# Operand sums of a fused attention and gated-FFN kernel put into other slots, and the products that read them started five slots later

## The chip, the cores and the metric

The kernel runs on one core of one Trainium2 chip. The metric is the device time of an execution in microseconds; the median of several runs counts.

## The reference, cut to what matters

```python
B, N, C = (4, 6016, 256)                      # attention over channels
qn = q / (np.linalg.norm(q, axis=1, keepdims=True) + 1e-06)
kn = k / (np.linalg.norm(k, axis=1, keepdims=True) + 1e-06)
s = kn.transpose(0, 2, 1) @ qn / tau          # 256 x 256 scores of a batch
a = np.exp(s - s.max(-1, keepdims=True))
a /= a.sum(-1, keepdims=True) + 1e-09
x = (v @ a).reshape(B * N, C)                 # 24064 tokens, d_ff = 1536
gate = 1.0 / (1.0 + np.exp(-(x @ w_gate)))
out = (gate * (x @ w_val)) @ w_out
```

## The kernel before, in words

The rows of a batch are 47 tiles of 128 (NT), taken as 12 chunks of four tiles (the last has three). For each batch the kernel needs the softmaxed 256 x 256 scores first. It multiplies them into the gate and value weights (`gh`, tiles gh_G and gh_H), so that each chunk of transposed v goes straight to the gate and value products.

A chunk has 12 **slots**, one for each block f of 128 of the 1536 hidden columns. A slot is a pass through `glu`: TensorE computes ps_gate and ps_val (two matmuls of 512 columns each), ScalarE takes the tanh of ps_gate into g_sb (L681), and VectorE forms hT from g_sb and ps_val (L682). ps_gate and ps_val have two buffers each. In the same slot `run_work` issues a twelfth of the output product of the chunk before. That product is done with seven block products in place of eight, in the manner of Strassen; its left operands are sums of blocks of hT, formed on VectorE by `a_sum` (L704). The tables `OWN_SLOTS` and `NEXT_SLOTS` name their slots: 7 to 11 of the chunk itself and 1, 3, 4, 5 and 6 of the next. Slots 0 and 2 have none. ScalarE copies a finished output product out of its bank (L758, L765), and GpSimd (POOL) adds its blocks up (L759, L760, L775, L776).

While batch b runs through its 12 x 12 slots, `side_work(b)` hangs the preparation of batch n = b + 1 onto them: `at(slot, ...)` places a call after the work of that slot, counted from the start of the batch. For n = 1 the scores are plain products. For n = 2 and 3, prepared while batches 1 and 2 run, they too are done with seven products in place of eight, in six **groups** of eight row tiles (the last has seven), 16 slots apart; s0 is the first slot of a group (0, 16, 32, 48, 64, 80).

- `load_qk` loads a group's q and k (tile qk_sb, four buffers) 24 slots ahead, from POOL's queue.
- `score_sums` forms the operand sums of a group, tiles qs0 to qs4. m = 0, 2, 3 and 4 run on VectorE (L351, L359, L364), each with one buffer; m = 1 is a copy by DMA (L355) and an adding DMA (`score_sum_q`, L369), with two buffers.
- `queue_scores` puts the group's products (28, or 25 in the last group; 128 columns each) on a list, and `run_scores` issues them over the next 16 slots: one in each of the first four slots, then two. They go into two PSUM banks, ps_s0 and ps_s1 (bank 0 and 1), in the order of the products: the first two to bank 0, then three to bank 1, then two to bank 0.
- `acc_square`, `acc_add` and `acc_fold` (L297, L308, L315) gather the squares for the norms.

After slot 98 of the batch come the end steps of the scores: `score_out` copies a bank to sm_sb on ScalarE (L426), `norms_mm` writes the norms into the free region of bank 1, and `root_seed`, `norms_inv`, `score_blocks`, `exps` and `gh` follow.

The order of every engine's instructions is the order in which the program issues them; nothing is scheduled again. The functions that the change touches, and their callers:

Of the kernel before, what the change touches and what calls it, by code (L numbers as in the profile page):

```python
# [46 lines left out]
    (1, "x2"), (1, "y2"), (1, "z2"), (1, "v2"),  # L47
)
NEXT_SLOTS = {1: 1, 3: 3, 4: 2, 5: 0, 6: 4}
OWN_SLOTS = {7: 1, 8: 3, 9: 2, 10: 0, 11: 4}  # L50


@with_exitstack
def kernel(
# [31 lines left out]
    FC = DFF // P  # L86
# [77 lines left out]
    t0, nt = groups0[0]  # L164
# [528 lines left out]
    def a_sum(b, ci, g, m):  # L693

        nt = groups[ci][1]
        half = nt // 2
        hT = hts[b, ci]
        if (b, ci, g) not in sums:
            sums[b, ci, g] = spool.tile(
                [P, len(A_SUMS), FC // 4, CH // 2], BF16, tag=f"s{g}", name="sums", bufs=2 - g  # L700
            )
        (r0, k0), op, (r1, k1) = A_SUMS[m]
        f0, f1 = g * (FC // 2), (g + 1) * (FC // 2)
        nc.vector.tensor_tensor(  # L704
            out=sums[b, ci, g][:, m, :, : half * P],
            in0=hT[:, f0 + k0 : f1 : 2, ds(r0 * half * P, half * P)],
            in1=hT[:, f0 + k1 : f1 : 2, ds(r1 * half * P, half * P)],
            op=op,
        )
# [94 lines left out]
    def run_work(work, share):  # L804

        upto = sum(w[0] for w in work) * share
        done = 0
        while work and done < upto:
            cost, fn, *args = work.pop(0)
            fn(*args)  # L810
            done += cost

    def store():
        while stores:
            b, ci = stores.pop(0)
            t0, nt = groups[ci]
            nc.sync.dma_start(out=out_rows[b][:, t0 : t0 + nt, :], in_=ffn.pop((b, ci))[:, :nt, :])
# [112 lines left out]
    def side_work(b):  # L930


        side = {}

        def at(slot, fn, *a):
            side.setdefault(divmod(slot, FC), []).append((fn, a))

        for ci in range(NCH):
            nb, nci = (b, ci + 1) if ci + 1 < NCH else (b + 1, 0)
            lb, lci = (b, ci + 2) if ci + 2 < NCH else (b + 1, ci + 2 - NCH)  # L940
            if nb < B:
                at(ci * FC + 2, transpose_v, nb, nci)
            if lb < B:
                at(ci * FC + (10 if (b, ci) == (0, 0) else 0), load_v, lb, lci)
            if (b, ci) == (0, 0):
                for i in range(FC // TPC):
                    at(8, copy_w_out, i)
                for n, m in enumerate((1, 0, 3, 2, 4)):
                    for i in range(FC // TPC):
                        at(11 + 2 * n, sum_w_out, m, i)  # L950
        n = b + 1
        if n == B:
            return side
        first, last = (14 if b == 0 else 0), 8 * FC
        wide = [(t, min(2 * TPC, NT - t)) for t in range(0, NT, 2 * TPC)]
        at(first, acc_start, n)
        for g, (t0, nt) in enumerate(groups if b == 0 else []):
            s0 = first + g * (last - first) // NCH
            at(max(FC - 3, s0 - 12), load_qk, n, t0, nt)
            for u in range(nt):  # L960
                at(first + (t0 + u) * (last - first) // NT, score, n, t0, u)
            for w in range(2):
                at(s0 + 1 + 4 * w, narrow_square, n, g, w)
                slot = s0 + 3 + 4 * w
                at(slot + 2 if w == 0 and slot % FC == 8 else slot, narrow_add, n, g, w)
        step = (last - first) / len(wide)
        for g, (t0, nt) in enumerate(wide if b else []):
            s0 = first + int(g * step)
            halves = [(0, nt - TPC), (TPC, TPC)]
            if s0 >= 24:  # L970
                at(s0 - 24, load_qk, n, t0, nt)
            for i in range(4):
                at(s0 + 3 * i, acc_square, n, t0, 1 - i // 2, halves, i % 2)
            for w in range(2):
                at(s0 + 11 - 6 * w, acc_add, n, t0, w, halves)
            for m in (0, 2, 3, 4):
                at(s0 + 3 * max(0, m - 1), score_sums, n, t0, m, halves)
            ahead = 0 if g == 0 else 5
            at(s0 + 1 - ahead, score_sums, n, t0, 1, halves)
            at(s0 + 6 - ahead, score_sum_q, n, t0, halves)  # L980
            end = first + int((g + 1) * step) + 3
            at(s0 + 3, queue_scores, n, t0, halves)
            for slot in range(s0 + 3, end):
                at(slot, run_scores, s0 + 3, end, slot)
        if n + 1 < B:
            for g, (t0, nt) in enumerate(wide[:2]):
                at(NCH * FC - 24 + 16 * g, load_qk, n + 1, t0, nt)
        s0 = 8 * FC + 2
        if b == 0:
            at(s0, acc_fold, n, 0, (2, 1))  # L990
            at(s0 + 1, acc_fold, n, 1, (2, 1))
            at(s0 + 3, norms_mm, n)
            at(s0 + 4, root_seed, n)
            at(s0 + 4, root_steps, n)
            at(s0 + 10, norms_inv, n)
            at(s0 + 11, spread_both, n)
            at(s0 + 13, read_row, n)
        else:
            at(s0 - 3, acc_fold, n, 1, (4,))
            at(s0 - 2, acc_fold, n, 1, (2, 1))  # L1000
            at(s0, acc_fold, n, 0, (4,))
            at(s0 + 2, acc_fold, n, 0, (2, 1))
            at(s0 + 5, score_out, n, 0)
            at(s0 + 6, norms_mm, n)
            at(s0 + 7, score_out, n, 1)
            at(s0 + 7, root_seed, n)
            at(s0 + 7, root_steps, n)
            at(s0 + 12, norms_inv, n)
            at(s0 + 12, spread_both, n)
            at(s0 + 14, read_row, n)  # L1010
            at(s0 + 14, score_blocks, n)
        at(s0 + 22, scale_x, n, 0)
        at(s0 + 24, scale_x, n, 1)
        at(s0 + 25, exps, n, 0)
        at(s0 + 26, exps, n, 1)
        at(s0 + 28, all_sums, n)
        at(s0 + 28, gh_tiles, n)
        for i, piece in enumerate(gh_order):
            slot = s0 + 29 + 2 * i
            if slot < NCH * FC:  # L1020
                at(slot, gh, n, piece, *((pss, "s"), (psm, "m"))[i % 2])
            else:
                spill.setdefault((n, *divmod(slot - NCH * FC, FC)), []).append((gh, (n, piece, psm, "m")))
        return side
# [12 lines left out]
    for b in range(B):  # L1037
        side = side_work(b)
        for ci in range(NCH):
            final = (b, ci) == (B - 1, NCH - 1)  # L1040
            for f in range(FC):
                mid = gh_mid.get(f) if (b, ci) == (0, 0) else None
                glu(b, ci, f, None if mid is None else (lambda: gh_pieces(mid)))
                if prev is not None:
                    if f == 4:
                        store()
                    if f + final in NEXT_SLOTS and prev != (0, 0):
                        a_sum(*prev, 1, NEXT_SLOTS[f + final])
                    run_work(work, 1 / max(1, FC - final - f))
                if f in OWN_SLOTS and not final and (b, ci) != (0, 0):  # L1050
                    a_sum(b, ci, 0, OWN_SLOTS[f])
                for fn, a in spill.get((b, ci, f), []) + side.get((ci, f), []):
                    fn(*a)
                if (b, ci) == (0, 0):
                    gh_pieces(gh_end.get(f, ()))
            prev = (b, ci)
            if not final:
                work = out_work(*prev)
# [39 lines left out]
```

## Time and profile before

| | us |
|---|---|
| median of 4 runs | 802.71 |
| lowest and highest | 800.45, 806.15 |
| the profiled execution, its own time | 800.45 |
| its span, first to last instruction | 798.7 |
| TensorE matmul busy | 778.7 (97%) |
| VectorE (DVE) busy | 712.9 (89%) |
| ScalarE (ACT) busy | 525.3 (66%) |
| GpSimd (POOL) busy | 398.6 (50%) |

Times in the profile are in microseconds from the first instruction, unless marked ns. Batch 1 runs from about 229.6 to 421.5 us and batch 2 to 613.4 us; these are the two in which the changed steps lie. The chain of work that ended last is followed back from the last instruction; in order of time its pieces have a start, a duration and what ran. A matmul's own duration contains its latency, so matmuls overlap in the trace; in the chain each counts only up to the start of the next. PE stands for TensorE, PEld for its weight loads, SP for SyncE.

### The profile page before, as it was taken

What the parts mean: (1) busy time and instruction counts of PE and PEld (TensorE: products, weight loads), DVE (VectorE), ACT (ScalarE), POOL (GpSimd) and SP (SyncE); (2) the same over time, 40 slices, a digit from 0 to 9 for tenths busy, and PEclk for the clock granted to TensorE, in tenths of its full rate; (3) what the DMA queues carried; (4) which work ended last, traced back from release to release, by engine and by line L of the source; (5) the groups of instructions that cost most, each with busy time, mean ns of one, the idle gap of its engine ahead of it and who ended that gap; (6) DMA issues with size and microseconds to landing.
All of it is one profiled execution on the core that took longest, in us unless ns stands there. A gap on an engine that the chain in (4) does not pass through costs nothing.

```text
span 798.7 us, 18203 instructions
## 1 busy us (share of the span) xinstructions
PE 778.7 (97%) x6861; PEld 498.0 (62%) x6875; DVE 712.9 (89%) x1228; ACT 525.3 (66%) x891; POOL 398.6 (50%) x618
## 2 busy tenths in 40 slices
PE   3899999999999999999999999999999999999998
PEld 2556666666666666666666666666666566666666
DVE  5768999999979999999988999999998898998996
ACT  3766777766667767676667777766666566665664
POOL 3565545446453566565843565655744244444433
PEclk9999999999999999999999999999999999999999
DMA  9997758532777899882577599967234323423402
GB/s 213 201 199 133 131 95 139 94 67 54 134 141 143 168 173 165 184 139 54 111 135 152 127 177 192 180 130 135 58 63 86 67 55 80 75 60 72 82 27 74
DMA packets 82776, 95.16 MB, mean 119 GB/s; under 512 B 52512, under 2 KB 58528, under 8 KB 82688
## 3 DMA queue, kind: packets, MB, share of 16 engines
q0 software_dynamic: 25616, 55.85, 39.8%
q1 hardware_dynamic: 56496, 37.30, 21.2%
q8 instruction: 53, 0.87, 0.4%
q10 hardware_dynamic: 576, 0.85, 0.3%
q14 instruction: 35, 0.29, 0.1%
HBM read 79.04 MB, written 24.64 MB: 130 GB/s over the span
## 4 chain that ended last, share of the span: by engine, by line
PE 95%; DMA 4%; issue 0%; DVE 0%; ACT 0%; POOL 0%; DVEq 0%; POOLq 0%
PE ps_gate L129 31%; PE ps_val L129 31%; PE ps_o L129 28%; DMA qk_sb<-in_k_dram 4%; PE ps_s L129 4%; PE ps_gh L129 2%; PE ps_end L129 0%; PE ps_n L129 0%; DVE x_sb L543 0%; PE ps_r L129 0%; ACT e_sb L561 0%; POOL qk_sb L148 0%; DVE x_sb L555 0%; DVE end L839 0%; DVE r L526 0%
## 5 line engine op out<-in xcount | busy, mean ns | idle before, releaser
L681 ACT ACTIVATE g_sb<-ps_gate 128x512 f32<-128x512 f32 (+1 forms) x576 | 337.9, 589 | 224.4 <-PE ps_gate L129 213.9
L682 DVE SCALAR_TENSOR_TENSOR hT<-g_sb,ps_val 128x512 bf16<-128x512 f32 (+1 forms) x576 | 385.4, 670 | 67.3 <-ACT g_sb L681 52.4
L129 PE MATMUL ps_gate<-vT,gh_G 128*128 128x512 bf16 (+1 forms) x1152 | 337.6, 375 | 0.1
L129 PE MATMUL ps_val<-vT,gh_H 128*128 128x512 bf16 (+1 forms) x1152 | 337.5, 375 | 0.0
L704 DVE TENSOR_TENSOR sums<-hT 128x768 bf16<-128x768 bf16 (+1 forms) x460 | 283.3, 616 | 0.0
L129 PEld LDWEIGHTS <-sums 128*128 128x128 bf16 x2670 | 183.0, 98 | 82.0
L129 PEld LDWEIGHTS <-gh_H 128*128 128x128 bf16 x1152 | 112.7, 98 | 130.8 <-issue 0.5
L775 POOL TENSOR_TENSOR out_sb<-out_sb,m_sb 128x256 f32<-128x256 f32 x89 | 79.0, 887 | 187.8 <-ACT out_sb L765 164.7
L129 PE MATMUL ps_o<-w_sums,sums 128*128 128x128 bf16 x1602 | 154.3, 219 | 0.0
L129 PEld LDWEIGHTS <-hT 128*128 128x128 bf16 x1200 | 88.3, 98 | 46.8
L759 POOL TENSOR_TENSOR m_sb<-m_sb 128x128 f32<-128x128 f32 x89 | 45.7, 513 | 126.5 <-ACT m_sb L758 126.1
L129 PEld LDWEIGHTS <-gh_G 128*128 128x128 bf16 x1152 | 92.5, 98 | 12.2 <-DVE gh_G L629 0.3
L129 PE MATMUL ps_o<-w_out_sb,sums 128*128 128x128 bf16 x1068 | 96.2, 219 | 0.0
L129 PE MATMUL ps_o<-w_sums,hT 128*128 128x128 bf16 x1068 | 95.5, 219 | 0.0
L776 POOL TENSOR_TENSOR out_sb<-out_sb 128x256 f32<-128x256 f32 x89 | 76.0, 854 | 7.0
L765 ACT COPY out_sb<-ps_o 128x512 f32<-128x512 f32 x89 | 52.2, 586 | 11.1 <-PE ps_o L129 8.8
L760 POOL TENSOR_TENSOR m_sb<-m_sb 128x128 f32<-128x128 f32 x89 | 55.8, 627 | 7.0
L129 PE MATMUL ps_s<-qk_sb 128*128 128x256 bf16 (+1 forms) x194 | 34.8, 298 | 15.5 <-DMA qk_sb<-in_k_dram 8.6
L758 ACT COPY m_sb<-ps_o 128x384 f32<-128x384 f32 x89 | 42.6, 479 | 3.6 <-PE ps_o L129 1.1
L257 ACT ACTIVATE sq<-qk_sb 128x1024 bf16<-128x1024 bf16 (+3 forms) x36 | 35.6, 1009 | 12.0 <-DMA qk_sb<-in_k_dram 11.9
L297 ACT ACTIVATE sq<-qk_sb 128x1024 bf16<-128x1024 bf16 (+1 forms) x40 | 41.2, 1031 | 0.2 <-DMA acc<-sq 0.2
L129 PEld LDWEIGHTS <-qk_sb 128*128 128x128 bf16 x286 | 27.0, 104 | 21.3 <-issue 10.2
(102 smaller groups left out, 443.4 us busy)
## 6 DMA issues: line engine op xcount, KB each, us to landing
out_dram<-out_sb SPq DMA_DIRECT2D x43, 512.0 KB, 3.4
v_sb<-in_v_dram POOLq DMA_DIRECT2D x44, 256.0 KB, 5.4
acc<-sq POOLq DMA_DIRECT2D x16, 512.0 KB, 8.0
qk_sb<-in_q_dram POOLq DMA_DIRECT2D x14, 512.0 KB, 10.3
qk_sb<-in_k_dram POOLq DMA_DIRECT2D x14, 512.0 KB, 8.4
qs<-qk_sb POOLq DMA_DIRECT2D x20, 256.0 KB, 5.2
qk_sb<-in_q_dram POOLq DMA_DIRECT2D x15, 256.0 KB, 4.7
qk_sb<-in_k_dram POOLq DMA_DIRECT2D x15, 256.0 KB, 6.9
```

Of the source, the lines that this page charges most:

```text
L129: nc.tensor.matmul(out, lhsT=lhsT, rhs=rhs, start=start, stop=stop, **kw)
L257: nc.scalar.activation(out=sq[:, :nt, :], in_=src[:, :nt, :], func=ACT.Square)
L297: nc.scalar.activation(out=s["sq", w][:, u0 : u0 + n, :], in_=src[:, u0 : u0 + n, :], func=ACT.Square)
L681: nc.scalar.activation(out=g_sb[:, :n], in_=ps_gate[:, :n], func=ACT.Tanh, scale=0.5)
L682: nc.vector.scalar_tensor_tensor(out=hts[b, ci][:, f, :n], in0=g_sb[:, :n], scalar=1.0, in1=ps_val[:, :n], op0=ALU.add, op1=ALU.mult,)
L704: nc.vector.tensor_tensor(out=sums[b, ci, g][:, m, :, : half * P], in0=hT[:, f0 + k0 : f1 : 2, ds(r0 * half * P, half * P)], in1=hT[:, f0 ...
L758: nc.scalar.copy(m, states[p]["ps"][:, : 3 * P].rearrange("p (n c) -> p n c", c=P))
L759: nc.gpsimd.tensor_tensor(out=m[:, 1, :], in0=m[:, 1, :], in1=m[:, 2, :], op=ALU.add)
L760: nc.gpsimd.tensor_tensor(out=m[:, 2, :], in0=m[:, 1, :], in1=m[:, 0, :], op=ALU.add)
L765: nc.scalar.copy(o[:, p : p + half + 1 : half, :], states[p]["ps"].rearrange("p (t c) -> p t c", c=C),)
L775: add(out=ends, in0=ends, in1=states[p]["m"][:, 1:3, :], op=ALU.add)
L776: add(out=ends, in0=ends, in1=mids, op=ALU.subtract)
```

## The change: three tables and offsets

It moves steps to other slots. A new table `SCORE_SLOTS`, chosen by the group's s0 modulo 12, gives the slots after s0 of the VectorE sums m = 0, 2, 3, 4; before they were at 0, 3, 6 and 9 after s0 in every group. A group's score products are queued and issued from slot s0 + 8 on, in place of s0 + 3, again over 16 slots. At the end of a batch's scores, bank 1 is copied out at slot 103 and bank 0 at slot 105, in place of the other order; `norms_mm` stays between them. The DMA steps (m = 1, loads, the adding of squares) stay where they are.

```diff
+SCORE_SLOTS = {0: (0, 2, 12, 14), 4: (2, 8, 10, 13), 8: (4, 6, 9, 12)}
...
-            for m in (0, 2, 3, 4):
-                at(s0 + 3 * max(0, m - 1), score_sums, n, t0, m, halves)
+            for m, slot in zip((0, 2, 3, 4), SCORE_SLOTS[s0 % FC]):
+                at(s0 + slot, score_sums, n, t0, m, halves)
             ahead = 0 if g == 0 else 5
             at(s0 + 1 - ahead, score_sums, n, t0, 1, halves)
             at(s0 + 6 - ahead, score_sum_q, n, t0, halves)
-            end = first + int((g + 1) * step) + 3
-            at(s0 + 3, queue_scores, n, t0, halves)
-            for slot in range(s0 + 3, end):
-                at(slot, run_scores, s0 + 3, end, slot)
+            end = first + int((g + 1) * step) + 8
+            at(s0 + 8, queue_scores, n, t0, halves)
+            for slot in range(s0 + 8, end):
+                at(slot, run_scores, s0 + 8, end, slot)
...
-            at(s0 + 5, score_out, n, 0)
+            at(s0 + 5, score_out, n, 1)
             at(s0 + 6, norms_mm, n)
-            at(s0 + 7, score_out, n, 1)
+            at(s0 + 7, score_out, n, 0)
```

In the last hunk s0 is 98, not a group's first slot.

## The prediction

> **What bounds the kernel now.** I read the busy shares first, then the chain of work that ended last, then what TensorE waited for.
>
> ```profile
> PE 778.7 (97%) x6861; PEld 498.0 (62%) x6875; DVE 712.9 (89%) x1228; ACT 525.3 (66%) x891; POOL 398.6 (50%) x618
> ...
> PE 95%; DMA 4%; issue 0%; DVE 0%; ACT 0%; POOL 0%; DVEq 0%; POOLq 0%
> ```
>
> The second line is the one that counts: 95% of the chain is TensorE work and 4% the first loads. DVE is 89% busy and has 0% of the chain. The waits of TensorE (who waited for what; us in total, times, longest) are all in the head of the run, before 37 us:
>
> ```profile
> PE ps_s L129 <- DMA qk_sb<-in_k_dram: 8.6, 6, 3.1
> PE ps_s L129 <- ACT qk_sb L195: 6.9, 1, 6.9
> PE ps_r L129 <- ACT e_sb L561: 0.7, 1, 0.7
> PE ps_rk L129 <- DVE r L527: 0.3, 1, 0.3
> ```
>
> The same question for 229 to 600 us, the two batches that the change touches, is answered with no row. Matmul ends are modelled, so a short stall can hide in a long matmul. I therefore compared pieces of the chain (start, duration, what) slot by slot. This is the worst chunk, 326.99 to 343.4 us:
>
> ```profile
> 328.36 0.43 PE ps_gate L129 x2
> 328.79 0.43 PE ps_val L129 x2
> 329.22 0.39 PE ps_o L129 x7
> 329.61 0.11 PE ps_s L129 x2
> ...
> 331.95 0.39 PE ps_o L129 x7
> 332.34 0.03 issue
> 332.37 0.27 PE ps_s L129 x2
> 332.64 0.43 PE ps_gate L129 x2
> 333.08 0.48 PE ps_val L129 x2
> ```
>
> A normal slot is 0.43 + 0.43 + 0.39 + 0.11 = 1.36 us. The slot from 331.09 has 0.03 of issue and a score piece of 0.27 in place of 0.11; the next val pair has 0.48 in place of 0.43: 0.24 us lost. The cause is on DVE, in the timeline:
>
> ```profile
> 330.53 1.79 DVE L364 TENSOR_TENSOR qs<-qk_sb 128x1024 bf16<-128x1024 bf16 x1
> ...
> 332.24 1.27 DVE L682 SCALAR_TENSOR_TENSOR hT<-g_sb,ps_val 128x512 bf16<-128x512 f32 x2
> ```
>
> An operand sum ran 1.79 us while two POOL adds (L775 at 330.74, L776 at 331.84) were active, the L682 behind it came late, and ps_val, which has two buffers, was not free. Stepping from gate pair to gate pair through both batches I find one more such place, 0.18 us near 518 us, and twice 0.05 us near 232 and 424 us. That is **0.5 us in all**. The check: seven chunks from 245.8 to 359.5 us last 16.24 us each; their work is 48 matmuls of 512 columns (24 pairs x 0.433 = 10.39), 84 output products (12 x 0.39 = 4.70) and some 21 score products (21 x 0.056 = 1.18), together 16.27. There is no room for more.
>
> **What the Trainium skill says.** "Perfetto Trace Analysis", Identifying the Most-Contended Engine: matmul busy share is no measure of distance from the limit. The trace agrees: a 512-column matmul has a mean of 375 ns in its row, yet a pair advances the chain by 0.43 us. "TensorE: Matmul & The Clock Gate", Back-to-back issue gap: the isolated gap is N/2.4 + 2.5 ns, 216 and 56 ns here; the trace has 0.43/2 and 0.39/7, so TensorE issues at that rate. (The same section's lower sustained figure for 512 columns, and its higher one for 128, don't show here.) "SBUF — State Buffer", Who interferes with whom: a DVE instruction with two SBUF inputs contends with a GpSimd instruction that reads SBUF. The trace agrees: these rows span a factor of 2.6 between median and longest, while L682, which has one input in PSUM, stays at a mean of 670.
>
> ```profile
> L364 DVE TENSOR_TENSOR qs<-qk_sb x28: 351/678/1794, 240.9 to 544.9; 128x1024 bf16<-128x1024 bf16 x20, 128x384 bf16<-128x384 bf16 x4, 128x512 bf16<-128x512 bf16 x4
> L351 DVE TENSOR_TENSOR qs<-qk_sb x12: 682/885/1217, 231.7 to 532.2; 128x1024 bf16<-128x1024 bf16 x10, 128x768 bf16<-128x768 bf16 x2
> L359 DVE TENSOR_TENSOR qs<-qk_sb x12: 677/684/1081, 235.8 to 536.4; 128x1024 bf16<-128x1024 bf16 x10, 128x768 bf16<-128x768 bf16 x2
> ```
>
> **The change, part by part.** No instruction is added or removed. The built order of POOL and SP, with all their DMA issues, is the same before and after; on ACT only two pairs of copies change places.
>
> 1. *Operand sums (52 DVE instructions).* Net time on DVE, start to start: L682 0.61 (237.68 to 238.29 us), an L704 sum of the output product 0.47 (330.06 to 330.53), a score sum 0.60 (240.95 to 241.55). A slot with L682 and L704 takes 1.08 of 1.36: 0.28 spare. With a score sum on top it takes 1.68: DVE falls 0.32 behind and catches up in little over a slot. In slots 0 and 2 of a chunk, which have no L704, a score sum makes 1.21: still 0.15 spare. By the tables, score sums in such slots go from 4 to 16 of 24 a batch; the other 8 stay beside an L704 (slots 5, 6, 8). So DVE's lag goes down. DVE isn't on the chain, so this is worth only the stalls that the lag causes: at most 0.24 + 0.18 us. Some can come back elsewhere: slot 92 of a batch now holds L682, L704 and two short score sums (0.61 + 0.47 + 0.27 + 0.34 = 1.69), and an acc fold follows in slots 95, 96 and 98 (0.60 net for its long step). By the same adding, the lag there peaks near 0.35 us, some 0.4 more with a POOL add over it, under the cushion of L682. That cushion is 1.2 us: L681 starts 0.2 us after its gate pair, so 0.63 into a slot, takes 0.60, L682 0.03 later takes 0.68, done at 1.94; the ps_val that needs its buffer starts two slots on, at 2 x 1.36 + 0.43 = 3.15. Value taken: -0.3 us; ends -0.5 and +0.7 (three stalls of the worst size seen).
>
> 2. *Score products five slots later (330 matmuls).* The same products at 0.056 us each, so 0 in sum. In a batch's first five affected slots some 6 products (0.34 us) go missing and the end has them instead. Cover: in slots 3 to 7 DVE also loses two score sums (1.2 us), so it isn't squeezed; in slots 99 to 103 TensorE has 0.06 to 0.11 us a slot more, which gives DVE time. Do operands come in time? run_scores takes one product in each of the first four slots, then two. The sum m=4 is first used 16 slots into its group and made at 12, 13 or 14 (before: 11 and 9): at least two slots, 2.7 us, as before. m=0 has 4 or more, m=2 6, m=3 4. The POOL-issued DMAs for m=1 gain five slots. Buffers: qs0 is next written at slot 16 and last read at 13; a qk_sb tile is last read at 23 and loaded again at 40. No wait appears; cost 0.
>
> 3. *Copies swapped.* Bank 0 now gets its last product in slot 103 and is copied in 105; bank 1 is complete by slot 100 and copied in 103. L426 (0.47 to 0.58 us) waits for nothing before. New is that norms_mm, which writes bank 1 in slot 104, waits for the copy of slot 103. Behind it on TensorE stands all of slot 105. Price: ACT starts the gate's L681 some 0.2 us after the pair, takes 0.59, then the copy 0.5: done 1.3 us after the pair's end, while norms_mm comes 2.2 us after it or later. Cost 0; if ACT were held up by a whole copy, 0.1 to 0.5 us, twice.
>
> Sum: -0.3 + 0 + 0 = **-0.3 us** on the profiled execution of 800.45 us (span 798.7 and 1.75 around it). That execution is the fastest of the four shown and 0.3% under their median of 802.71; against the median I say 802.4.
>
> **Rivals.**
>
> *A, no change* (above): 802.4, between 801.5 and 803.5 by its own costs, wider by the scatter of runs.
>
> *B, faster.* The median is 2.3 us above the profiled run. If that gap is the same DVE stall in other executions, the change could take it too: 800.4, or -0.3%. For it: such stalls depend on where POOL adds fall, and that can vary. Against: the trace shows only 0.5 us of them, and TensorE's sum of work leaves no others. Past -0.5% (4 us) nothing in the trace reaches.
>
> *C, slower: the sums meet POOL.* Slots 0 and 2 are where the second pair of POOL adds (L775, L776) runs, for its ACT copy ends as a chunk begins: from 230.05 to 231.58 us in the chunk at 229.8, and from 330.74 in the one at 326.99. A score sum wholly beneath them takes 1.1 us longer. One hit in slot 0 or 2 puts DVE 0.95 behind, inside the cushion of 1.2; two, in slots 0 and 2 of one chunk, make 0.95 - 0.28 + 0.95 = 1.6, and 0.4 us stall. In all twelve groups that is 4.8 us: 807.5. It decides once both sums of a chunk are hit. Against: the pair lasts 1.5 to 2.2 us and the two slots lie 2.7 us apart, so mostly one is hit; and before, too, POOL adds met score sums.
>
> *D, it doesn't do what it says*: a third of the score sums still stand beside an L704, and the old stalls stay: 802.7.
>
> **How the numbers follow.** About 0.5% (4 us) is what a measurement of this kernel can tell from no change. A 0.73 and D 0.10 lie within it; B 0.09, of which 0.03 for a time past 4 us from a cause unseen; C 0.08, of which 0.05 past 4 us and 0.03 with only some chunks hit. So faster 0.03, same 0.73 + 0.10 + 0.06 + 0.03 = 0.92, slower 0.05. The range takes B's 800.4 and half of C, and the scatter of the four runs (800.45 to 806.15): 799.8 to 805.8.
>
> **What the profile after would show.** Right: TensorE still 95% of the chain; chunks of 16.2 us through both batches; L364's longest well under 1.79 us or without a late L682 behind it; no TensorE wait for L426. Wrong: a row of TensorE waiting for hT L682, qs or sm_sb; score-batch chunks longer than 16.4 us; or the whole chain shorter by more than 0.5 us, which would mean that TensorE's matmul spacing itself had changed.

## The result, and the profile after

The changed kernel takes 803.56 us (median of 35 runs, 802.72 to 807.72); the kernel before takes 801.93 us in 56 runs (799.85 to 806.15). The ratio is 1.0024, with a 95% interval of 1.0017 to 1.0031: **slower by some 1.9 us** (the medians as they stand differ by 1.6). The time is within the forecast range and within the 0.5% that was called no change, but it moved the other way from the forecast gain, and clear of the noise.

The profiled execution of the changed kernel has a span of 802.5 us. These are the busy shares and the shares of the chain of work that ended last:

```profile
PE 781.6 (97%) x6861; PEld 498.5 (62%) x6875; DVE 716.3 (89%) x1228; ACT 525.4 (65%) x891; POOL 396.7 (49%) x618
...
PE 89%; DVE 4%; DMA 4%; issue 1%; POOL 1%; ACT 0%; DVEq 0%; POOLq 0%
```

The busy line says next to nothing: 97% as before. The chain says it: VectorE, which had 0%, has 4%, and TensorE went from 95% to 89%. (A share of the chain is not a loss: 4% of it is 32 us.) The waits of TensorE and of its weight loads in the two batches (231 to 617 us; total, times, longest), where the kernel before had no row for matmuls and 0.6 us for weight loads, are:

```profile
PEld L131 <- issue: 3.7, 7, 0.6
PE ps_val L131 <- DVE hT L684: 1.8, 6, 0.4
PEld L131 <- DVE sums L706: 1.1, 4, 0.4
```

(The change adds two lines near the top of the file, so L684 is the former L682, L706 the former L704, L366 the former L364.) Stepping from one chunk's first gate product to the next, as the prediction did, gives nearly the whole of it. From the first gate product of batch 1 to that of batch 3 pass 383.80 us before and 386.29 after. After the change the stalls are in the same places of both batches, all but one:

| us lost by TensorE (slots counted from 0) | before, batch 1 / 2 | after, batch 1 / 2 |
|---|---|---|
| chunk 0, slot 2 | 0.05 / 0.05 | 0.05 / 0.05 |
| chunk 3, slot 3 | - | 0.11 / - |
| chunk 3, slot 11 | - | 0.34 / 0.34 |
| chunk 5, slot 11 | - / 0.18 | - |
| chunk 6, slots 3 and 4 | 0.24 / - | - |
| chunk 7, slot 11 | - | 0.51 / 0.51 |
| chunk 8, slot 2 | - | 0.51 / 0.50 |
| sum of both | 0.5 | 2.9 |

So the old stalls went, as forecast, and larger ones came. The profiled execution also reached batch 1 1.4 us later (231.0 in place of 229.6 us), 1.0 us of it lost in slots 1 and 3 of batch 0, where the listed waits are for the load of w_gate; a second profile of the same kernel (below) didn't.

How the stall at the end of chunk 3 arises can be read in VectorE's timeline (start, duration). The group with s0 = 32 has its m=4 sum in slot 44 of the batch, slot 8 of chunk 3, behind an L706. VectorE runs more than a slot behind TensorE, so its work of slots 8 and 9 falls into TensorE's slots 9 to 11:

```profile
291.67 0.68 DVE L684 SCALAR_TENSOR_TENSOR hT<-g_sb,ps_val 128x512 bf16<-128x512 f32 x1
292.27 0.80 DVE L706 TENSOR_TENSOR sums<-hT 128x768 bf16<-128x768 bf16 x1
292.99 1.21 DVE L366 TENSOR_TENSOR qs<-qk_sb 128x1024 bf16<-128x1024 bf16 x1
294.12 0.67 DVE L684 SCALAR_TENSOR_TENSOR hT<-g_sb,ps_val 128x512 bf16<-128x512 f32 x1
```

POOL's timeline at the same time, with the idle time before the first add and what ended it:

```profile
291.93 0.72 POOL L777 TENSOR_TENSOR out_sb<-out_sb,m_sb 128x256 f32<-128x256 f32 x1 [2.01 <-ACT out_sb L767]
292.72 0.92 POOL L778 TENSOR_TENSOR out_sb<-out_sb 128x256 f32<-128x256 f32 x1
```

And TensorE's:

```profile
294.06 0.59 PE L131 MATMUL ps_gate<-vT,gh_G 128*128 128x512 bf16 x2
294.84 0.59 PE L131 MATMUL ps_val<-vT,gh_H 128*128 128x512 bf16 x2 [0.19 <-DVE hT L684]
```

L706 takes 0.80 in place of 0.55 and L366 1.21 in place of 0.68, for 0.25 + 0.53 = 0.78 us, while the adds run. The L684 behind them ends at 294.79, and the ps_val that needs its buffer starts at 294.84. Without the wait it would have started one gate pair later than 294.06, at 294.49: 0.35 us late. The profile's own figure of 0.19 is smaller, since the matmul before it ends later by its latency.

The stall in slot 11 of chunk 7 is the same thing with the last group's m=4, two short sums, in slot 92 of the batch. VectorE (the two sums are one line, from the start of the first to the end of the second), POOL and TensorE:

```profile
356.80 0.67 DVE L684 SCALAR_TENSOR_TENSOR hT<-g_sb,ps_val 128x512 bf16<-128x512 f32 x1
357.39 0.91 DVE L706 TENSOR_TENSOR sums<-hT 128x768 bf16<-128x768 bf16 x1
358.22 1.21 DVE L366 TENSOR_TENSOR qs<-qk_sb 128x384 bf16<-128x384 bf16 x2
359.36 0.67 DVE L684 SCALAR_TENSOR_TENSOR hT<-g_sb,ps_val 128x512 bf16<-128x512 f32 x1
```

```profile
357.16 0.73 POOL L777 TENSOR_TENSOR out_sb<-out_sb,m_sb 128x256 f32<-128x256 f32 x1 [1.28 <-ACT out_sb L767]
357.96 0.92 POOL L778 TENSOR_TENSOR out_sb<-out_sb 128x256 f32<-128x256 f32 x1
```

```profile
360.08 0.59 PE L131 MATMUL ps_val<-vT,gh_H 128*128 128x512 bf16 x2 [0.36 <-DVE hT L684]
```

Before VectorE has won that back, the long step of acc_fold (L317) of slot 95 meets the next pair of adds, and TensorE waits again in slot 2 of chunk 8. VectorE, POOL and TensorE in turn:

```profile
362.09 0.82 DVE L706 TENSOR_TENSOR sums<-hT 128x768 bf16<-128x768 bf16 x1
362.83 1.21 DVE L317 TENSOR_TENSOR acc<-acc 128x1024 bf16<-128x1024 bf16 x1
363.97 0.68 DVE L684 SCALAR_TENSOR_TENSOR hT<-g_sb,ps_val 128x512 bf16<-128x512 f32 x1
```

```profile
361.77 0.73 POOL L777 TENSOR_TENSOR out_sb<-out_sb,m_sb 128x256 f32<-128x256 f32 x1 [2.88 <-ACT out_sb L767]
362.58 0.93 POOL L778 TENSOR_TENSOR out_sb<-out_sb 128x256 f32<-128x256 f32 x1
```

```profile
364.70 0.59 PE L131 MATMUL ps_val<-vT,gh_H 128*128 128x512 bf16 x2 [0.36 <-DVE hT L684]
```

Here ps_val starts 0.95 after its gate pair (363.75) in place of 0.43. Before the change the same acc_fold step, under the same pair of adds, took 1.22 us as well, and no wait followed:

```profile
360.43 1.22 DVE L315 TENSOR_TENSOR acc<-acc 128x1024 bf16<-128x1024 bf16 x1
```

```profile
360.21 0.89 POOL L775 TENSOR_TENSOR out_sb<-out_sb,m_sb 128x256 f32<-128x256 f32 x1 [2.53 <-ACT out_sb L765]
361.18 1.06 POOL L776 TENSOR_TENSOR out_sb<-out_sb 128x256 f32<-128x256 f32 x1
```

But VectorE came to it 0.9 us sooner: it started 0.93 us after the first gate product of chunk 8 (360.43 and 359.5), after the change 1.82 us (362.83 and 361.01), for the sums of slot 92 lay just before it.

### The profile page after: what moved, and what is told of

It reads as the page before. It is cut to its first block, busy times and chain, and to the rows that moved or that the text cites. A ratio compares the mean times of both kernels' runs of the same rounds, so it can differ in the third digit from the quotient of the medians.

```text
span 802.5 us, 18203 instructions
## 1 busy us (share of the span) xinstructions
PE 781.6 (97%) x6861; PEld 498.5 (62%) x6875; DVE 716.3 (89%) x1228; ACT 525.4 (65%) x891; POOL 396.7 (49%) x618
## 4 chain that ended last, share of the span: by engine, by line
PE 89%; DVE 4%; DMA 4%; issue 1%; POOL 1%; ACT 0%; DVEq 0%; POOLq 0%
PE ps_val L131 29%; PE ps_gate L131 28%; PE ps_o L131 26%; PE ps_s L131 4%; DMA qk_sb<-in_k_dram 3%; PE ps_gh L131 2%; DVE hT L684 2%; DVE sums L706 1%; DMA w_gate<-in_moe_w_gate_dram 1%; DVE qs L366 1%; ACT g_sb L683 0%; DVE acc L317 0%; POOL w_gate L210 0%; POOL w_val L210 0%; POOL qk_sb L150 0%
## 5 line engine op out<-in xcount | busy, mean ns | idle before, releaser
L684 DVE SCALAR_TENSOR_TENSOR hT<-g_sb,ps_val 128x512 bf16<-128x512 f32 (+1 forms) x576 | 385.7, 670 | 66.6 <-ACT g_sb L683 54.6
L706 DVE TENSOR_TENSOR sums<-hT 128x768 bf16<-128x768 bf16 (+1 forms) x460 | 286.2, 622 | 0.0
L761 POOL TENSOR_TENSOR m_sb<-m_sb 128x128 f32<-128x128 f32 x89 | 43.9, 493 | 132.0 <-ACT m_sb L760 131.7
L762 POOL TENSOR_TENSOR m_sb<-m_sb 128x128 f32<-128x128 f32 x89 | 56.9, 639 | 7.0
```

The costliest lines, as they stand in the source:

```text
L684: nc.vector.scalar_tensor_tensor(out=hts[b, ci][:, f, :n], in0=g_sb[:, :n], scalar=1.0, in1=ps_val[:, :n], op0=ALU.add, op1=ALU.mult,)
L706: nc.vector.tensor_tensor(out=sums[b, ci, g][:, m, :, : half * P], in0=hT[:, f0 + k0 : f1 : 2, ds(r0 * half * P, half * P)], in1=hT[:, f0 ...
L761: nc.gpsimd.tensor_tensor(out=m[:, 1, :], in0=m[:, 1, :], in1=m[:, 2, :], op=ALU.add)
L762: nc.gpsimd.tensor_tensor(out=m[:, 2, :], in0=m[:, 1, :], in1=m[:, 0, :], op=ALU.add)
```

## The experiments

The theory: the loss is TensorE's waits for VectorE, and they come from where the new table puts the score sums, in front of and under POOL's adds. The rivals: 1, the later products; 2, the time lost before batch 1 (the expectations give it as 1.3 us); 3, too many instructions on VectorE, adds or not; 4, the order of the copies. "Batches" below is the time from the first gate product of batch 1 to that of batch 3 in the profile (383.80 before, 386.29 after); "stalls" is TensorE's loss in it. Kernels run together shared the runs of the kernel before.

**Sums back at the old slots, the rest changed**

```diff
-SCORE_SLOTS = {0: (0, 2, 12, 14), 4: (2, 8, 10, 13), 8: (4, 6, 9, 12)}
+SCORE_SLOTS = {0: (0, 3, 6, 9), 4: (0, 3, 6, 9), 8: (0, 3, 6, 9)}
```

> The changed kernel with the VectorE sums back at 0, 3, 6 and 9 slots after s0; products still from slot 8 on, copies still swapped. Theory (the table is the cause: VectorE falls behind at the ends of chunks 3 and 7 and in chunk 8, and TensorE waits some 1.4 us a batch): the waits of the changed kernel at those places go, ratio to before 1.000 (0.9990 to 1.0010). Rival 1 (the later products are the cause: TensorE's slots are shorter at the batch's start and longer at its end): ratio stays near 1.0024. Rival 2 (the 1.3 us more that the profiled execution lost before 231 us is the cause, not the score batches): ratio stays near 1.0024 too, with no stall in the score batches.

Ratio 1.0011 (1.0001 to 1.0020), batches 384.72 us, stalls 1.4 us. The stalls at the ends of chunks 3 and 7 and in chunk 8 are gone, so they come from the table. But 0.9 us remain, outside what the theory gave: with the old table the later products do cost something. Both batches lose 0.16 us in slot 9 of chunk 0 and 0.25 in slot 0 of chunk 1. TensorE (first two lines) and VectorE there:

```profile
245.44 0.59 PE L131 MATMUL ps_gate<-vT,gh_G 128*128 128x512 bf16 x2
246.14 0.59 PE L131 MATMUL ps_val<-vT,gh_H 128*128 128x512 bf16 x2
```

```profile
244.81 0.68 DVE L366 TENSOR_TENSOR qs<-qk_sb 128x1024 bf16<-128x1024 bf16 x1
245.41 0.68 DVE L684 SCALAR_TENSOR_TENSOR hT<-g_sb,ps_val 128x512 bf16<-128x512 f32 x1
```

ps_val starts 0.70 after its gate pair and 0.05 after the L684 ends. In the kernel before, the same L366 and L682 started at 244.76 and 245.36, so VectorE is no later here. TensorE is earlier: it went from slot 0 to slot 9 of the batch in 12.05 us, before in 12.45. These 0.4 us are seven missing products (7 x 0.056), and they come back as 0.41 us of waiting. Batch 1 also lost 0.43 us in slots 1 and 2 of chunk 6, the chunk in which the kernel before lost its 0.24.

**One sum moved: m=4 of the groups with s0 % 12 = 8 from slot 8 of a chunk to slot 3**

```diff
-SCORE_SLOTS = {0: (0, 2, 12, 14), 4: (2, 8, 10, 13), 8: (4, 6, 9, 12)}
+SCORE_SLOTS = {0: (0, 2, 12, 14), 4: (2, 8, 10, 13), 8: (4, 6, 9, 7)}
```

> The changed kernel with one number of the table altered: in groups with s0 % 12 = 8 the sum m=4 comes 7 slots after s0 (slot 3 of a chunk) in place of 12 (slot 8 of a chunk). Theory in its narrow form (the sum in slot 8, followed by three more slots with sums of the output product and by the POOL adds, is what spends VectorE's cushion): the waits of 0.34 us at the end of chunk 3 and 0.51 us at the end of chunk 7 go, chunk 8's 0.51 shrinks; TensorE stalls in the two batches from 2.8 to under 1.3 us; ratio 1.0003 to 1.0013. Rivals 1 and 2: ratio stays near 1.0024.

Ratio 1.0008 (0.9996 to 1.0020), batches 384.75 us, stalls 1.4 us. The waits in slot 11 of chunks 3 and 7 and in slot 2 of chunk 8 are gone. In their place are 0.18 and 0.12 in slot 3 of chunk 3, 0.30 in its slot 8 and 0.11 in slot 8 of chunk 7: the sums in slots 3 and 5 now follow one another too closely. More than half of the loss went with one number: the place of this one sum was worth 1.5 us; the forecast end of 1.3 us of stalls was missed by little.

**The changed kernel without POOL's two adds**

```diff
+            if b not in (1, 2):
-            add(out=ends, in0=ends, in1=states[p]["m"][:, 1:3, :], op=ALU.add)
-            add(out=ends, in0=ends, in1=mids, op=ALU.subtract)
+                add(out=ends, in0=ends, in1=states[p]["m"][:, 1:3, :], op=ALU.add)
+                add(out=ends, in0=ends, in1=mids, op=ALU.subtract)
```

> The changed kernel without the two POOL adds behind each finished output product (L777, L778) in batches 1 and 2; the block sums of their outputs are left out. Theory (a sum that meets those adds runs up to twice as long, and only that makes the lag more than the cushion): VectorE's sums run at 0.55 and 0.68 us, no TensorE wait at the ends of chunks 3 and 7 nor in chunk 8, ratio 0.999 to 1.0003. Rival 3 (VectorE is overfull there by the number of its instructions alone): the wait in chunk 8 stays at 0.3 us or more, ratio above 1.001. Rivals 1 and 2: near 1.0024.

Ratio 0.9993 (0.9984 to 1.0002), batches 383.39 us, and of the stalls only the two of 0.05 us in chunk 0 are left. Rivals 1 to 3 fall for the changed kernel: the same VectorE instructions in the same order, with the products as late and the acc folds in place, no longer hold TensorE up. Leaving the adds out also frees POOL's queue earlier; that it is the lengthening of VectorE's sums that counts is read from the timelines, in which the ps_val waits for L684. The groups of the two batches (busy us, mean ns), with the adds (changed kernel) and then without:

```profile
L706 DVE TENSOR_TENSOR sums<-hT 128x768 bf16<-128x768 bf16 x220 | 140.9, 640 | 0.0
L366 DVE TENSOR_TENSOR qs<-qk_sb 128x1024 bf16<-128x1024 bf16 x20 | 17.2, 861 | 0.0
```

```profile
L706 DVE TENSOR_TENSOR sums<-hT 128x768 bf16<-128x768 bf16 x220 | 130.0, 591 | 0.0
L366 DVE TENSOR_TENSOR qs<-qk_sb 128x1024 bf16<-128x1024 bf16 x20 | 15.2, 760 | 0.0
```

The adds stretch them on the mean by only 49 and 101 ns. It is not the mean that costs 2.8 us but the few places where it falls together. The means without the adds are still above the 0.55 and 0.68 us that were expected, since the adds of m_sb (L761, L762) were left in: the 46 L706 that meet one of them have a median of 0.73 us.

**The copies in the old order, the rest changed**

```diff
-            at(s0 + 5, score_out, n, 1)
+            at(s0 + 5, score_out, n, 0)
             at(s0 + 6, norms_mm, n)
-            at(s0 + 7, score_out, n, 0)
+            at(s0 + 7, score_out, n, 1)
```

> The changed kernel with the bank copies in the old order (bank 0 at slot 103, bank 1 at 105). Theory: no effect, ratio 1.0024 as for the whole change, within 1.0015 and 1.0033, since no wait on L426 shows. Rival 4 (norms_mm held up by the copy): ratio 1.000.

Ratio 1.0037 (1.0025 to 1.0049), batches 386.30 us, stalls 2.9 us in the same places to within 0.03 us. The ratio, of six runs, is above the end that was given; the batches are not longer, so the order of the copies does nothing in them, and what the six runs lost elsewhere was not followed up. Rival 4 falls.

**The kernel before without the same two adds**

The edit is the same as two experiments above, in the kernel before.

> The kernel before, without the same two POOL adds (here L775, L776) in batches 1 and 2; the block sums of their outputs are left out. Theory (in both kernels only sums stretched by those adds make TensorE wait): the two stalls of 0.24 and 0.18 us go, the two batches last 383.3 us in place of 383.8, ratio 0.9985 to 1.0000, so that the whole loss of the change depends on the adds. Rival 3 (leaving the adds out frees as much in the kernel before as in the changed one): the batches shorten by some 2.9 us here too, ratio about 0.996.

In the profile the two stalls went: batches 383.45 us, stalls 0.18 us. So with the adds out, both kernels come to the same time (383.39 and 383.45), and the change's loss in these batches depends on the adds. The measured ratio, though, is 1.0018 (1.0002 to 1.0033), against the expectation. Of its 22 runs (800.27 to 808.45 us), the six that had a granted TensorE clock below 0.997 took 805.46 us or more; the other 16 have a median of 801.48, where the kernel before has 801.53. Why this kernel drew six of them, and the kernel before two in 59, stays open. The profile is what carries this experiment, not its time.

**Another row of the table: slots 10, 0, 2 and 6 of a chunk for the groups with s0 % 12 = 8**

```diff
-SCORE_SLOTS = {0: (0, 2, 12, 14), 4: (2, 8, 10, 13), 8: (4, 6, 9, 12)}
+SCORE_SLOTS = {0: (0, 2, 12, 14), 4: (2, 8, 10, 13), 8: (2, 4, 6, 10)}
```

> The changed kernel with the last row of the table replaced by 8: (2, 4, 6, 10), so that these groups' sums stand in slots 10, 0, 2 and 6 of a chunk, at least four slots apart where the slot has a sum of the output product. Theory (stalls come where a second score sum follows before VectorE has won back what the first and a pair of POOL adds cost): the waits at the ends of chunks 3 and 7 and in chunk 8 go or fall below 0.2 us each; the two batches last 383.3 to 384.3 us (386.3 for the changed kernel); ratio 0.9995 to 1.0010. Rival 1 (the later products): a loss as with the old slots, 384.7 us, ratio 1.001 or more.

Ratio 0.9987 (0.9978 to 0.9995), batches 383.56 us, stalls 0.26 us, of which 0.15 in slots 3 and 9 of chunk 3. The ratio is better than was forecast. TensorE's waits in the two batches, as listed by the profile, are down to these:

```profile
PEld L131 <- DVE sums L706: 0.4, 1, 0.4
PEld L131 <- issue: 0.4, 2, 0.2
```

With products as late and copies swapped as in the changed kernel, four other numbers in a table turn 0.24% slower into 0.13% faster. This version beats both kernels, by its 13 runs; the next but one, with the same table, comes out at 0.9994, not clear of no change.

**Old sum slots, and the first group's products from slot 4 on**

```diff
+            begin = s0 + (8 if g else 4)
-            at(s0 + 8, queue_scores, n, t0, halves)
-            for slot in range(s0 + 8, end):
-                at(slot, run_scores, s0 + 8, end, slot)
+            at(begin, queue_scores, n, t0, halves)
+            for slot in range(begin, end):
+                at(slot, run_scores, begin, end, slot)
```

> The kernel with the sums at the old slots, products from slot 8 on, copies swapped, but the products of a batch's first group from slot 4 on, spread over 20 slots. Theory (with the old slots, the later products took 0.34 us of TensorE work out of slots 3 to 8 of a batch, TensorE reached VectorE's late L684 that much earlier and waited 0.16 us in slot 9 and 0.25 us in slot 12 or 13): with 4 products (0.23 us) back in those slots the two waits shrink from 0.41 to about 0.2 us a batch; the two batches last 384.2 to 384.4 us (384.7 with all products from slot 8); ratio 1.0003 to 1.0010. Rival 5 (the waits come from something else in the shifted order): still 384.7 us.

TensorE's way from slot 0 to slot 9 took 12.28 us, between the 12.05 and 12.45 above, and the waits at the turn from chunk 0 to chunk 1 fell from 0.41 to 0.20 us in both batches: the working of this experiment is confirmed there. But the batches took 385.38 us, not 384.3, for batch 1 lost 0.96 us in slot 0 of chunk 5 and 0.51 in chunk 6, which batch 2 did not. Ratio 1.0007 (0.9998 to 1.0016). In chunk 5 POOL's queue had stood 7.1 us in front of L371, the DMA that adds q for m=1, and afterwards ran m_sb adds, output adds and loads one after the other; L706 took 1.17 us and L366 1.21 beneath them.

**Both: the row (2, 4, 6, 10), and the first group's products from slot 4 on**

> The changed kernel with the table's last row as 8: (2, 4, 6, 10) and the first group's products from slot 4 on over 20 slots. Theory: hardly any wait of TensorE left in the two batches, 383.3 to 384.0 us, ratio 0.999 to 1.0005; it can beat the kernel before by 0.5 us at most, which is within what the rounds can tell. Rival 1: 384.7 us.

Ratio 0.9994 (0.9987 to 1.0000), batches 383.51 us, stalls 0.23 us. With this table the earlier start adds nothing, since there was no wait left in chunks 0 and 1 for it to take.

**The three kernels profiled again**

> The kernel before, unchanged, profiled once more. If TensorE's waits in the two batches come from the fixed order of the instructions alone: the same 0.5 us in the same places (slots 75 and 76 of batch 1, slot 71 of batch 2), two batches in 383.8 us. If they depend on when a pair of POOL adds happens to start: another amount in other places, 383.4 to 385 us.

> The changed kernel, unchanged, profiled once more. Theory (the table puts sums under POOL adds whose times follow the same order each time): the waits at the ends of chunks 3 and 7 and in chunk 8 are there again within 0.05 us, the two batches last 386.3 us as in the two profiles with this table; the 1.3 us more before 231 us need not come again. Rival 2 (the loss sits before 231 us): batch 1 starts at 231 us again.

> The changed kernel with the row 8: (2, 4, 6, 10), profiled once more. Theory: TensorE's waits in the two batches stay under 0.5 us, 383.4 to 383.9 us. If its first profile was a lucky draw: 384.5 us or more.

The changed kernel repeats itself: batches 386.31 us, stalls 2.9 us in the same slots to within 0.03 us, and batch 1 starts at 229.4 us: the loss before it was one execution's, and rival 2 falls. The table (2, 4, 6, 10) takes 383.96 us, with 0.46 us in slot 3 of chunk 3 that had 0.08 the first time, a little over what was expected: the sum in slot 0 of that chunk (L361) took 1.55 us under the second pair of adds, the first time 1.16. The kernel before is the one that does not repeat: batches 384.80 us, with 1.37 us lost at once in slot 1 of chunk 6. POOL's timeline there:

```profile
325.07 0.91 POOL L369 DMA_DIRECT2D qs<-qk_sb  x1 [4.05 <-DMA qs<-qk_sb]
325.69 1.04 POOL L775 TENSOR_TENSOR out_sb<-out_sb,m_sb 128x256 f32<-128x256 f32 x1
326.82 0.94 POOL L776 TENSOR_TENSOR out_sb<-out_sb 128x256 f32<-128x256 f32 x1
...
328.32 1.03 POOL L775 TENSOR_TENSOR out_sb<-out_sb,m_sb 128x256 f32<-128x256 f32 x1
329.42 1.07 POOL L776 TENSOR_TENSOR out_sb<-out_sb 128x256 f32<-128x256 f32 x1
```

and VectorE's:

```profile
325.32 1.84 DVE L704 TENSOR_TENSOR sums<-hT 128x768 bf16<-128x768 bf16 x1
327.09 0.67 DVE L682 SCALAR_TENSOR_TENSOR hT<-g_sb,ps_val 128x512 bf16<-128x512 f32 x1
327.68 0.55 DVE L704 TENSOR_TENSOR sums<-hT 128x768 bf16<-128x768 bf16 x1
328.15 1.75 DVE L364 TENSOR_TENSOR qs<-qk_sb 128x1024 bf16<-128x1024 bf16 x1
```

POOL waited for the DMA of m=1 to land before it could issue the adding one, the adds queued behind it, and when it came free the first pair ran at once and the second 0.6 us behind it. An L704 and the L364 two slots later were stretched to 1.84 and 1.75 us. In the first profile the same wait of POOL ended at 327.70, the first pair of adds, from 328.33 to 330.18, lay over two L682 and an idle 0.55 us and stretched no sum, and only 0.24 us was lost to the second. That the time at which POOL came free made the difference is what the two timelines show together; nothing was run that moved it alone.

## Why the prediction was wrong

**The bound** was right: in the kernel before TensorE issues nearly all the time, and only stalls of a few tenths move the time. The measured 1.9 us lie between the two readings of the stalls: the batches are 2.5 us longer than in the first profile of before and 1.5 us longer than in its second.

**Step 1 failed, in the term "the lag there peaks near 0.35 us, some 0.4 more with a POOL add over it, under the cushion of L682".** The place that it names, slot 92, is slot 8 of chunk 7, and TensorE lost 0.51 us behind it. Take as lag by how much L684 starts later than 1.26 us after its gate pair (0.63 + 0.60 + 0.03, from the step's own sum). The first L684 behind the two sums, that of slot 9, started at 359.36, its gate pair at 356.51: a lag of 1.59 us, where the step had 0.35 + 0.4. Four things were off:

1. The lag doesn't start from zero. At slot 8 VectorE was still 0.33 us late from the sum in slot 5, so that even in the kernel without the adds the lag reaches 0.69 and not 0.35. The step saw that a slot with an L704 wins back only 0.28 us, yet counted sums beside an L704 (8 of 24 in place of 20) and not the distance between them: sums in slots 5 and 8 of a chunk are followed by L706 in slots 9, 10 and 11.
2. One pair of adds stretches two sums in succession, the L706 and the score sum behind it: 0.90 us more lag here than without the adds (0.78 at the end of chunk 3), not 0.4.
3. The cushion is smaller here: the slots last 1.31 us in place of 1.36, which takes it from 1.2 to 1.1 us, and 1.59 less 1.1 is the stall.
4. The acc fold of slot 95 was entered with 0.60 us; it took 1.21 beneath a pair of adds.

The stalls of 0.34, 0.51 and 0.51 us a batch are these. The upper end of that step (+0.7 us) stood on the worst stalls of a single execution, and one measured stall in another execution of the same kernel was 1.37 us.

**The gain in it was right**: the old stalls went, and the longest score sum fell from 1794 to 1209 ns, as the prediction wished to see. That sign was a poor one. The last rows answer to those shown of before:

```profile
L366 DVE TENSOR_TENSOR qs<-qk_sb x28: 410/679/1209, 249.1 to 552.1; 128x1024 bf16<-128x1024 bf16 x20, 128x384 bf16<-128x384 bf16 x4, 128x512 bf16<-128x512 bf16 x4
L353 DVE TENSOR_TENSOR qs<-qk_sb x12: 551/684/1193, 233.0 to 540.3; 128x1024 bf16<-128x1024 bf16 x10, 128x768 bf16<-128x768 bf16 x2
L361 DVE TENSOR_TENSOR qs<-qk_sb x12: 549/679/1198, 236.0 to 542.5; 128x1024 bf16<-128x1024 bf16 x10, 128x768 bf16<-128x768 bf16 x2
```

A sum of 1.2 us in a bad place costs more than one of 1.8 in a good one: in the changed kernel an L706 took 1.84 us at 326.10, and no stall followed. The sign that told is the row of TensorE waiting for hT. Chunks longer than 16.4 us told nothing: there is one of 16.63 (279.14 to 295.77) after the change, but before it, too, chunk 6 of batch 1 lasted 16.58.

**Step 2, cost 0**, held for the change as a whole: no wait for qs or qk_sb came, and with the new table the turn from chunk 0 to 1 has no stall. Its cover was the one that it named, the two score sums that slots 3 to 7 lose; with the old table, where slots 3 and 6 keep theirs, the same 0.4 us cost 0.41. The step did not work out the price without that cover.

**Step 3, cost 0**, held: 386.30 against 386.29 us.

**The rivals.** The right one was C, with the wrong place for most of the loss. It looked at the second pair of adds in slots 0 and 2, where a slot has time to spare. It was the first pair, over VectorE's work of slots 8 and 9, where every slot has an L706, and the second pair over the acc folds of the last group. Its own place, slot 0, cost 0.11 us in one batch after the change and 0.46 in one with the row (2, 4, 6, 10). The L684 of that slot starts 0.89 us late in any case, at 281.29 after 0.98 us of waiting for ScalarE's tanh, which the 0.15 us to spare of step 1 leaves out. Its example of a pair at 330.74 was not the usual time of such a pair: POOL's queue had waited 7.17 us, until 327.70, before the pair ahead of it. Its rule (two sums lengthened before the lag is won back) is what was seen, though at the ends of chunks 3 and 7 it was one pair that lengthened both. It was given 0.08 and a place where, by its own argument, two hits are rare.

**The base.** The prediction took 0.5 us as what this kernel loses. That was one execution; another lost 1.5 us. The extra 1 us shown there may be a part of the 1.5 us by which the median of 801.93 lies above the profiled 800.45. Rival B named this gap and dismissed it, since "the trace shows only 0.5 us of them". That a better table can take it is consistent with 0.9987 for the row (2, 4, 6, 10), whose first profile is only 0.24 us better than the first of before; that it is this part of the gap was not measured run by run.

## What to carry to other kernels

When the bound engine never waits and a second one is nearly as full, don't count how many slots are overloaded: carry the lag forward from slot to slot with what each slot wins back, and put two overloads at least as far apart as that takes. Look at which work of a third engine lies over these slots, for it can double what runs beneath it. And take the size of small stalls from two or three profiles of the same kernel, not from one.

## What was not expected of the hardware

One pair of POOL adds (1.6 to 2.2 us together) lengthened VectorE sums from 0.55 to as much as 1.90 (row (2, 4, 6, 10), at 324.17; no stall followed) and from 0.68 to 1.79 us. L682 and L684, with one input in PSUM, took at most 0.69 us under the same adds in four profiles (the kernel before twice, the changed one, the row (2, 4, 6, 10)). The factor of 2.6 in the prediction is that of the L364 row alone; its other two rows have 1.4 and 1.6. The Trainium skill, "SBUF — State Buffer", Summary: rules for kernel authors, says that of two such instructions the second to issue is fully blocked until the first finishes. The lengthening bears with this, but the order does not come out here: in the second profile of the kernel before, the L704 of 325.32 started 0.37 us before the add at 325.69 and yet took 1.84 us, and that add was lengthened as well, to 1.04 us from 0.72. POOL was still issuing a DMA when this sum started (325.07 to 325.98); whether that counts as coming first was not tested. Where a pair's time fell on two sums, they took 0.80 and 1.21.

And a wait in POOL's queue for a DMA to land (4.05 us in one profile of the kernel before, 7.17 in the other) moved the first pair of adds behind it by 3.1 us against TensorE's chunk, from 1.6 us before the first gate product of chunk 6 to 1.5 us after it. With the one went a loss of 1.37 us in that chunk, with the other 0.24, though POOL is busy for only half of the time.
